# A kernel of attention and two expert mixtures: stores on GpSimd's queue, a buffer for squares, another order of weight jobs

## The chip, the cores and the metric

The kernel runs on one core of a Trainium2 chip. The metric is the time of one execution on the device in microseconds. Before the change three runs took 1863.81, 1864.39 and 1872.37 us; their median is 1864.39 us. The execution that the profiler recorded took 1853.53 us.

## The reference

Windowed attention feeds a first mixture of eight experts, in which every token goes through every expert with a weight of its own, and its result feeds a second one, in which every token goes to exactly one expert.

```python
x = attention(q, k, v)                      # 4 x 576 tokens, 8 heads of 64, window of 64
# mixture 1: N = 2304 tokens, D = 512, F = 1024, E = 8
P = exp(x @ w_gate - max)                   # then 8 rounds of row and column scaling
for e in range(E):
    out += P[:, e:e+1] * (relu(x @ w1[e]) @ w2[e])
# mixture 2: tokens are assigned greedily by logit, N / E to an expert
for e in range(E):
    mask = assigned == e
    out2[mask] = relu(out[mask] @ w1[e]) @ w2[e]
```

## The kernel before

All matmuls of the experts run in float16 pairs: each float32 value is split into a high part (ScalarE, L345, a scaled copy) and a low part (VectorE, L347, the scaled value minus the high part), and a product takes three matmuls. Weights are scaled by a power of two first. For that the sum of squares of a weight set is taken (`sum_scale`): four squares on ScalarE (L287), each over 1024 columns, whose values nobody reads and whose row sums are kept, then a matmul with ones (L302) that sums over partitions.

The stages are: attention and the first expert of mixture 1 (to about 300 us of the span), experts 1 to 7 of mixture 1 (to about 1520 us), and mixture 2 with its routing. For experts 1 to 6 the products are Strassen's: a layer 1 step (L959) is 24 matmuls against quarter weights in `w1b` and `w1x`, and a layer 2 step (L1096) is 12 matmuls against `w2b` and others. The 18 token tiles form nine pairs k; layer 2 runs two pairs behind layer 1. Of each seven products of layer 2, VectorE adds three to the output `acc` (L1072); for the other four ScalarE writes a scaled copy `y` (L1077), and twice in each pair a DMA on GpSimd's queue adds `y` to `acc` (L1079). The first of the two goes to a tile whose other half VectorE still adds to, three products later.

Between the matmuls, weights are prepared in the background. `weights_all` works through a list of jobs: the w2 and the w1 of an expert of mixture 1, and w1 or w2 of experts of mixture 2. A job squares and splits the 2 MB that four loads brought to the one buffer `raw` (L1610), stores the split parts to DRAM, from where they are loaded when their expert comes, and loads the next job's weights as parts of `raw` become free. A split or a square takes one of four buffers named `st2k` in turn and waits until the store that last read it has landed. Stores of w1 are L427 (14 of 256 KB in a job), of mixture 2's weights L473 (8), of w2 L533 (14) and, for the last expert, L498 (8).

The loads of an expert's w1 are L454, seven of 512 KB into quarter slots. Each is issued when the whole w1 of that expert has been prepared (`w1p`) and the last product of the expert before that reads the slot has been written (`w1f`). The loads of w2 (L561) follow the same rule. The x parts of a pair are L909, 896 KB.

Instructions stand on each engine in the order in which the program writes them. The background advances by ticks: every twelve matmuls of layer 1 and every six of layer 2 give 0.7 ticks, and a job asks for so many ticks between its steps: 1.2 and 0.7 for the two halves of a split (`SPW`, `LOW`), 1.5 for a square, 3.0 for the matmul behind the squares, 11 from a load to the first use. All the loads and stores named so far stand on SP's queue in program order, except L1079. A DMA whose turn has not come holds up the DMAs behind it on its queue.

Of the kernel before, what the change touches and what calls it, by code (L numbers as in the profile page):

```python
# [9 lines left out]
F16 = mybir.dt.float16  # L10
I32 = mybir.dt.int32
AF = mybir.ActivationFunctionType
# [163 lines left out]
def body(ctx, tc, dims, q, k, v, wg1, w11, w12, wg2, w21, w22, wgT, out):  # L176
# [102 lines left out]
    def sum_scale(buf, inv, sc, key=None):  # L279


        mp = small.tile([128, 8], F32, name="np8")
        e = []
        wide = not bg.hold
        for c in range(4 if wide else 0):
            a = yield Rq("ACT", 1.4, [(key, c)] if key else [], wait=1.5)
            A.activation(st2k()[:, 0:1024], buf[:, c * 1024:(c + 1) * 1024], AF.Square, accum_out=mp[:, c:c + 1])  # L287
            e.append(a.end)
        for c in range(0, 0 if wide else 8, 2):
            kd = [(key, c // 2)] if key else []  # L290
            a = yield Rq("ACT", 0.8, kd, wait=1.3)
            junk = st2k() if "pool" in rc else acc[:, NT - 2].bitcast(F16)
            s0, s1 = [buf[:, x * 512:(x + 1) * 512] for x in (c, c + 1)]
            A.activation(junk[:, 0:512], s0, AF.Square, accum_out=mp[:, c:c + 1])
            d = yield Rq("DVE", 0.77, kd, wait=0)
            V.scalar_tensor_tensor(junk[:, 512:1024], s1, 1.0, s1, op0=OP.mult, op1=OP.mult, accum_out=mp[:, c + 1:c + 2])
            e += [a.end, d.end]
        m1 = small.tile([128, 1], F32, name="m1")
        p = yield Rq("PE", 0.2, e, "psb", wait=3.0)
        pt = psb.tile([128, 512], F32, name="pb")  # L300
        k = 4 if wide else 8
        PE.matmul(pt[:, 0:k], rc["ones"], mp[:, 0:k], start=True, stop=True)  # L302
        d = yield Rq("DVE", 0.9, [p.end])
        V.tensor_reduce(m1, pt[:, 0:k], AX.X, OP.add)
        norm_pow2(m1, sc, inv)
        fl.release("psb", p.idx, d.start + 0.3)
        rc["sct"] = d.end
# [69 lines left out]
    def strassen_w1(e, sc, free):  # L377
# [31 lines left out]
        else:  # L409
# [6 lines left out]
            def out(src, name):  # L416
                o = W1N.index(name) * 2048
                for c in range(2):
                    st = []

                    def two():
                        st.append(st2k()[:, 0:1024].rearrange("p (t x) -> p t x", t=2))
                        return st[0][:, 0], st[0][:, 1]

                    yield from split_f(src[:, c], two, None, sc, 512, wait=SPW)
                    d = w1scr[e * 128:(e + 1) * 128, o:o + 2048].rearrange("p (t x) -> p t x", t=2)
                    SP.dma_start(d[:, :, c * 512:(c + 1) * 512], st[0])  # L427

            yield from comb(t3, A11, A21, OP.subtract)
            yield from out(A22, "A22")  # L430
# [29 lines left out]
    def prep_moe2(e, m, free):  # L460
        sc = wsc()
        yield from sum_scale(raw, winv[:, 2 + m, e:e + 1], sc, "job")
        for c in range(8):
            a, cc = (c % 2, c // 2) if m == 0 else (c // 4, c % 4)
            st = []

            def two():
                st.append(st2k()[:, 0:1024].rearrange("p (t x) -> p t x", t=2))
                return st[0][:, 0], st[0][:, 1]

            x, y = yield from split_f(raw[:, c * 512:(c + 1) * 512], two, None, sc, 512, pool="st2k", wait=SPW if c else 1.0)
            d = wscr[m][a][e * 128:(e + 1) * 128, :].rearrange("p (t x) -> p t x", t=2)
            SP.dma_start(d[:, :, cc * 512:cc * 512 + 512], st[0])  # L473
            fl.release("st2k", x.idx, y.end + 4.6)
            if c % 2:
                free(c // 2)
# [10 lines left out]
    def prep_w2(e, free):  # L487
        yield from sum_scale(raw, winv[:, 1, e:e + 1], w2sc, "job")
        for c in range(8):
# [5 lines left out]
                return st[0][:, 0], st[0][:, 1]  # L495

            x, y = yield from split_f(raw[:, cs], two, None, w2sc, 512, pool="st2k", wait=SPW if c else 1.0)
            SP.dma_start(w2rows(e)[:, :, cs], st[0])  # L498
            fl.release("st2k", x.idx, y.end + 4.6)
            if c % 2:  # L500
                free(c // 2)
# [2 lines left out]
    def quarters_w2(e, free):  # L504
# [14 lines left out]
        def sp(src, name):  # L519
            o = QN.index(name) * 2048  # L520
            for c in range(2):
# [8 lines left out]
                x, y = yield from split_f(src[:, 2 * c:2 * c + 2], two, None, w2sc, 512, deps=[("w2", 0)] if e == 1 else (),  # L530
                                          pool=None if e == 1 else "st2k", wait=SPW)
                d = w2scr[e * 128:(e + 1) * 128, o:o + 2048].rearrange("p (t x) -> p t x", t=2)
                SP.dma_start(d[:, :, c * 512:(c + 1) * 512], st[0])  # L533
                fl.release("st2k", x.idx, y.end + 4.6)

        yield from comb(t3, B22, B12, OP.subtract)
# [677 lines left out]

    def held_weights():
        w2g = rc["pool"].tile([128, FC, E], F32, name="w2g")
        junk = rc["pool"].tile([128, DM], F16, name="junk")
        row = []
        for e in range(E + 1):
            if e < E:  # L1220
# [374 lines left out]

    jobs = []
    m2left = [(m, x) for x in range(E) for m in range(2)]
    for e in range(1, E):
        jobs += [(1, e), (0, e)]
        for _ in range(M2PLAN.get(e, len(m2left))):  # L1600
            m, x = m2left.pop(0)
            jobs.append((2 + m, x))
# [11 lines left out]
    def weights_all():  # L1614
        for r in range(4):
            load(0, r)
        for k, (m, e) in enumerate(jobs):
# [4 lines left out]
                bg.done.add("raw2")  # L1622
                return
            yield Idle(WAIT[m])
            while m >= 2 and "T" not in rc:
                yield IDLE
            if m >= 2:
                yield from prep_moe2(e, m - 2, free)
# [48 lines left out]
    def change():  # L1677
# [5 lines left out]
        rc["ones"] = rc["pool"].tile([128, 128], F32, name="ones")  # L1683
        V.memset(rc["ones"], 1.0)
        rc["tmp"] = rc["pool"].tile([128, 2, 512], F32, name="tmp")
        mpool = mid.enter_context(tc.tile_pool(name="mpool", bufs=1))
        rc["xr"] = mpool.tile([128, 3, 2 * XO], F16, name="xr")
        w1x = mpool.tile([128, 6144], F16, name="w1x")
# [171 lines left out]
```

## Time and profile before

| what | value |
|---|---|
| median of three runs | 1864.39 us |
| profiled execution | 1853.53 us |
| its span, first to last instruction | 1851.7 us |
| mean granted TensorE clock | 0.984 of full speed |
| TensorE matmul, busy | 1764.1 us, 95% |
| VectorE, busy | 1318.2 us, 71% |
| ScalarE, busy | 1048.8 us, 57% |
| GpSimd, busy | 203.7 us, 11% |
| DMA packets of the hardware queue | 286.75 MB, 45.8% of 16 engines |
| DMA packets of GpSimd's queue | 71.33 MB, 15.6% of 16 engines |

The span is the time between the first and the last instruction of one execution; about 2 us lie around it. In the rows below, PE is TensorE's matmul side, PEld its weight loads, DVE VectorE, ACT ScalarE, POOL GpSimd and SP SyncE; a letter q behind an engine means its queue or sequencer. "out<-in" are names of the program's buffers: `ws` and `w1scr`, `w2scr` are the prepared weights in DRAM, `xr` the x parts, `in_moe_w` the weights as given.

### The profile page before, as it was taken

To read this page: it belongs to the slowest core of one execution; us is meant where nothing else is said; L and a number is where in the kernel's file an instruction comes from. 1 tells how busy PE (TensorE), PEld (TensorE's weight loads), DVE (VectorE), ACT (ScalarE), POOL (GpSimd) and SP (SyncE) were. 2 spreads that over 40 slices of the span, in tenths; PEclk is the share of its full clock that TensorE was granted. 3 is DMA by queue.
4 is the path that set the end of the run, shared out by engine and by line. 5 is a ranking of instruction groups with operands and counts; after the bars stand their busy time and mean duration, and the time that the engine had idled before them with its cause. 6 is when DMAs were issued, how large, how long until landed. Compare 5 with 4: busy or idle time off the path is not lost.

```text
span 1851.7 us, 51111 instructions
## 1 busy us (share of the span) xinstructions
PE 1764.1 (95%) x21427; PEld 1496.2 (81%) x21427; DVE 1318.2 (71%) x3129; ACT 1048.8 (57%) x2045; POOL 203.7 (11%) x268
## 2 busy tenths in 40 slices
PE   6999999998999999999999999999999999799997
PEld 5766556997899989998999899899887774577776
DVE  7888955787588778867887787678567737566640
ACT  6776335765676767677667676677643432122222
POOL 0000000000000000000010000000100102323231
PEclk9999999999999999999999999999999999799999
DMA  7353427766786997689769678986962201535460
GB/s 220 116 172 104 142 80 253 237 194 202 263 247 186 297 307 214 193 250 323 217 178 325 210 214 260 307 261 171 298 210 75 75 24 53 197 130 192 147 234 26
DMA packets 183447, 361.35 MB, mean 195 GB/s; under 512 B 15728, under 2 KB 105072, under 8 KB 179120
## 3 DMA queue, kind: packets, MB, share of 16 engines
q1 hardware_dynamic: 159984, 286.75, 45.8%
q0 software_dynamic: 23232, 71.33, 15.6%
q8 instruction: 168, 2.75, 0.6%
q14 instruction: 63, 0.52, 0.1%
HBM read 232.31 MB, written 97.40 MB: 178 GB/s over the span
## 4 chain that ended last, share of the span: by engine, by line
PE 70%; DVE 12%; DMA 12%; issue 3%; ACT 3%; SPq 0%; POOL 0%; POOLq 0%; DVEq 0%; ACTq 0%
PE p L959 14%; PE p L1096 12%; PE pb L959 10%; PE pb L1096 8%; PE p L1521 5%; PE p L1124 4%; DMA ws<-st2k 3%; PE p L1146 3%; PE p L823 3%; PE p L1507 3%; DMA raw<-in_moe_w_dram 2%; PE pb L1352 1%; DMA w2b<-w2scr 1%; DMA acc<-y 1%; DVE st2k L347 1%
## 5 line engine op out<-in xcount | busy, mean ns | idle before, releaser
L959 PEld LDWEIGHTS <-w1b 128*128 128x128 f16 x6048 | 361.5, 99 | 24.4 <-DMA w1b<-w1scr 10.3
L959 PEld LDWEIGHTS <-w1x 128*128 128x128 f16 x4536 | 270.4, 98 | 17.3 <-issue 9.7
L1096 PEld LDWEIGHTS <-hall 128*128 128x128 f16 x2268 | 214.9, 98 | 29.5 <-issue 4.7
L1096 PEld LDWEIGHTS <-xh 128*128 128x128 f16 x2268 | 214.7, 98 | 23.3 <-DVE xh L1037 1.0
L1079 POOL DMA_DIRECT2D acc<-y x108 | 93.2, 863 | 1095.3 <-ACT y L1077 672.9
L959 PE MATMUL p<-xr,w1b 128*128 128x128 f16 x3024 | 192.3, 220 | 14.3 <-DMA w1b<-w1scr 10.0
L959 PE MATMUL p<-xr,w1x 128*128 128x128 f16 x3024 | 191.2, 220 | 5.2 <-ACT xl L976 4.6
L347 DVE SCALAR_TENSOR_TENSOR st2k<-raw,wsc,st2k 128x512 f16<-128x512 f32 x200 | 148.5, 748 | 60.0 <-ACT st2k L345 57.3
L959 PE MATMUL pb<-xr,w1b 128*128 128x128 f16 x3024 | 190.3, 219 | 0.0
L345 ACT ACTIVATE st2k<-raw,wsc 128x512 f16<-128x512 f32 x200 | 140.0, 713 | 53.2 <-DMA ws<-st2k 41.3
L979 DVE TENSOR_TENSOR xl<-pb,xl 128x512 f32<-128x512 f32 x126 | 86.7, 688 | 92.7 <-PE pb L959 80.1
L1077 ACT ACTIVATE y<-p,SE 128x256 f32<-128x256 f32 x216 | 101.3, 469 | 82.4 <-PE p L1096 76.5
L287 ACT ACTIVATE st2k<-raw 128x1024 f16<-128x1024 f32 x108 | 113.5, 1052 | 43.9 <-DMA raw<-in_moe_w_dram 17.2
L1072 DVE SCALAR_TENSOR_TENSOR acc<-pb,SE,acc 128x256 f32<-128x256 f32 x162 | 77.9, 481 | 61.8 <-PE pb L1096 38.6
L1124 PE MATMUL p<-w2b,hall 128*128 128x512 f16 x432 | 107.1, 384 | 0.0
L823 PE MATMUL p<-xh,w1b 128*128 128x384 f16 (+1 forms) x512 | 99.7, 286 | 3.6 <-DVE w1b L347 1.6
L976 ACT ACTIVATE xl<-p 128x512 f32<-128x512 f32 x126 | 74.3, 590 | 50.5 <-PE p L959 50.5
L959 PE MATMUL pb<-xr,w1x 128*128 128x128 f16 x1512 | 94.8, 219 | 3.3 <-ACT xl L976 3.3
L1146 PE MATMUL p<-w2b,hall 128*128 128x512 f16 x432 | 97.2, 379 | 0.0
L823 PEld LDWEIGHTS <-w1b 128*128 128x128 f16 x768 | 63.2, 98 | 36.1 <-issue 3.9
L1096 PE MATMUL p<-w2b,hall 128*128 128x256 f16 x648 | 79.7, 273 | 5.6 <-ACT y L1077 3.3
L1096 PE MATMUL p<-w2b,xh 128*128 128x256 f16 x648 | 81.6, 275 | 0.3 <-DVE xh L1033 0.3
(322 smaller groups left out, 3323.0 us busy)
## 6 DMA issues: line engine op xcount, KB each, us to landing
raw<-in_moe_w_dram SPq DMA_DIRECT2D x128, 512.0 KB, 7.2
xr<-xtd SPq DMA_DIRECT2D x63, 896.0 KB, 6.5
ws<-st2k SPq DMA_DIRECT2D x128, 256.0 KB, 6.3
acc<-y POOLq DMA_DIRECT2D x108, 256.0 KB, 6.2
w1scr<-st2k SPq DMA_DIRECT2D x84, 256.0 KB, 2.8
w2scr<-st2k SPq DMA_DIRECT2D x78, 256.0 KB, 4.0
w2b<-w2scr SPq DMA_DIRECT2D x28, 512.0 KB, 8.3
w1b<-w1scr SPq DMA_DIRECT2D x24, 512.0 KB, 9.7
```

The lines of the kernel that those rows point to most:

```text
L287: A.activation(st2k()[:, 0:1024], buf[:, c * 1024:(c + 1) * 1024], AF.Square, accum_out=mp[:, c:c + 1])
L345: A.activation(hi, src, AF.Copy, scale=sc)
L347: V.scalar_tensor_tensor(lo, src, sc, hi, op0=OP.mult, op1=OP.subtract)
L823: PE.matmul(p[:, 0:w], w1v[wi][:, c, fs], x[:, c, ts], start=(n == 0), stop=(n == 3 * DC - 1))
L959: PE.matmul(bank[:, fs], aq[wi][:, c, fs], xq[xi][:, c], start=(start and f == 0 and m == 0), stop=(m == 5), skip_group_check=True)
L979: V.tensor_tensor(t, bank, t, OP.add)
L1077: A.activation(y[:, h * hd:(h + 1) * hd], bank[:, 0:hd], AF.Copy, scale=SE[:, e, i:i + 1])
L1079: G.dma_start(acc[:, i], y, accum_op=OP.add)
L1096: PE.matmul(bank[:, 0:hd], hq[hi][:, c], wv[wi][:, c], start=(pool is not None and m == 0), stop=(m == 11), skip_group_check=True)
L1124: PE.matmul(s[0], h[hi].rearrange("p (c t) -> p c t", c=4)[:, f % 4], w2v[wi][:, f], start=(f == 0 and hi == wi == 0), stop=(f == FC - 1 a ...
L1146: PE.matmul(p, h[:, f, js], w2v[wi][:, f], start=(n == 0), stop=(n == 3 * FC - 1))
L1521: PE.matmul(p[:, 0:CAP], wv2[f // 4][w][:, f % 4, dsl], x[:, f], start=(n == 0), stop=(n == 3 * FC - 1))
```

## The change

Every store of prepared weights is issued on GpSimd's queue in place of SP's, 304 DMAs. The squares of a job write one buffer `junk` of their own in place of an `st2k` buffer, and the matmul behind them is asked for 3.6 ticks later in place of 3.0. The scratch of the last expert's gate products (`held_weights`) takes the first tile of `y` in place of memory of its own. The list of jobs is ordered anew: it begins with w2 and w1 of experts 1 and 2, and then each expert's share of mixture 2's jobs follows w2 and w1 of the expert after it. The test that keeps mixture 2's jobs from starting before the shared buffers exist now holds for every job from the third on.

```diff
@@ sum_scale
-            A.activation(st2k()[:, 0:1024], buf[:, c * 1024:(c + 1) * 1024], AF.Square, accum_out=mp[:, c:c + 1])
+            A.activation(rc["junk"], buf[:, c * 1024:(c + 1) * 1024], AF.Square, accum_out=mp[:, c:c + 1])
...
-        p = yield Rq("PE", 0.2, e, "psb", wait=3.0)
+        p = yield Rq("PE", 0.2, e, "psb", wait=3.6)
@@ strassen_w1
-                    SP.dma_start(d[:, :, c * 512:(c + 1) * 512], st[0])
+                    G.dma_start(d[:, :, c * 512:(c + 1) * 512], st[0])
@@ prep_moe2
-            SP.dma_start(d[:, :, cc * 512:cc * 512 + 512], st[0])
+            G.dma_start(d[:, :, cc * 512:cc * 512 + 512], st[0])
@@ prep_w2
-            SP.dma_start(w2rows(e)[:, :, cs], st[0])
+            G.dma_start(w2rows(e)[:, :, cs], st[0])
@@ quarters_w2
-                SP.dma_start(d[:, :, c * 512:(c + 1) * 512], st[0])
+                G.dma_start(d[:, :, c * 512:(c + 1) * 512], st[0])
@@ held_weights
-        junk = rc["pool"].tile([128, DM], F16, name="junk")
+        junk = rc["y"][:, 0].bitcast(F16)[:, 0:DM]
@@ the list of jobs
+    jobs += [(1, 1), (0, 1)]
     for e in range(1, E):
-        jobs += [(1, e), (0, e)]
+        if e < E - 1:
+            jobs += [(1, e + 1), (0, e + 1)]
@@ weights_all
-            while m >= 2 and "T" not in rc:
+            while k >= 2 and "T" not in rc:
@@ change
+        rc["junk"] = rc["pool"].tile([128, 1024], F16, name="junk")
```

On SP, at the boundary from expert 1 to expert 2 of mixture 1, before (L1610 loads raw, L454 loads the next w1):

```order
L427 DMA w1scr<-st2k 128x2x512 x6
L909 DMA xr<-xtd 128x3584
L427 DMA w1scr<-st2k 128x2x512 x8
L1610 DMA raw<-in_moe_w_dram 128x1024 x4
L454 DMA w1b<-w1scr 128x2048 x2
L454 DMA w1x<-w1scr 128x2048
L454 DMA w1b<-w1scr 128x2048
L454 DMA w1x<-w1scr 128x2048 x2
L454 DMA w1b<-w1scr 128x2048
L909 DMA xr<-xtd 128x3584
```

and at the same place after the change (raw is now loaded in L1612):

```order
L1612 DMA raw<-in_moe_w_dram 128x2x512 x3
L909 DMA xr<-xtd 128x3584
L454 DMA w1b<-w1scr 128x2048 x2
L454 DMA w1x<-w1scr 128x2048
L454 DMA w1b<-w1scr 128x2048
L1612 DMA raw<-in_moe_w_dram 128x2x512
L454 DMA w1x<-w1scr 128x2048
L1612 DMA raw<-in_moe_w_dram 128x2x512
L454 DMA w1x<-w1scr 128x2048
L454 DMA w1b<-w1scr 128x2048
```

The stores of that w1 are gone from SP, and its loads no longer stand behind them and four raw loads, but among the raw loads of a later job.

On GpSimd, all of experts 1 to 6 of mixture 1, before (`mmg` is the maximum that starts the gates, L1204 a subtraction of the last expert's stage):

```order
L268 ISA mmg<-m1g 128x1
L1079 DMA acc<-y 128x512 x108
L1204 ISA
L1204 TENSOR_TENSOR st2k<-tmp,st2k 128x512 x8
L1233 ISA
```

and after the change, of the same stretch only the work of expert 1 up to its seventh pair:

```order
L533 DMA w2scr<-st2k 128x2x512 x6
L1079 DMA acc<-y 128x512
L533 DMA w2scr<-st2k 128x2x512 x5
L1079 DMA acc<-y 128x512
L533 DMA w2scr<-st2k 128x2x512 x3
L1079 DMA acc<-y 128x512 x2
L427 DMA w1scr<-st2k 128x2x512 x2
L1079 DMA acc<-y 128x512
L427 DMA w1scr<-st2k 128x2x512 x4
L1079 DMA acc<-y 128x512
L427 DMA w1scr<-st2k 128x2x512 x4
L1079 DMA acc<-y 128x512
```

Two to six stores now stand between one acc<-y and the next, where none stood.

On ScalarE, at a job's last split and first squares, before (np holds the row sums, `w2sc` and `wsc` a scale):

```order
L345 ACTIVATE st2k<-raw,wsc 128x512
L973 ACTIVATE xl<-p_9527 128x512
L287 ACTIVATE st2k,np_9834<-raw 128x1024
L1077 ACTIVATE y<-p_9564,SE 128x256
L287 ACTIVATE st2k,np_9834<-raw 128x1024
```

and after:

```order
L345 ACTIVATE st2k<-raw,w2sc 128x512
L1077 ACTIVATE y<-p_9843,SE 128x256
L976 ACTIVATE xl<-p_10155 128x512
L287 ACTIVATE junk,np_10152<-raw 128x1024
L1077 ACTIVATE y<-p_10182,SE 128x256
```

The squares stand where they stood between evacuations, but they write `junk` and no buffer that a store reads.

## Rows read from the trace of the kernel before

**Rows 1.** First part of the page: busy us (share of the span) xinstructions.
```profile
PE 1764.1 (95%) x21427; PEld 1496.2 (81%) x21427; DVE 1318.2 (71%) x3129; ACT 1048.8 (57%) x2045; POOL 203.7 (11%) x268
```

**Rows 2.** Table by stretches: stretch, us, busy of each engine, PEclk, DMA share, GB/s.
```profile
300.00:454.40 154.40, 152.03 (x2120) 143.53 (x2118) 120.91 (x193) 105.80 (x175) 11.46 (x13) 1.00 0.70 211
454.40:464.40 10.00, 0.01 (x1) 0.01 (x1) 0.79 (x1) 0.47 (x1) 0.86 (x1) 0.76 0.97 319
464.40:470.00 5.60, 5.60 (x42) 4.86 (x43) 0.00 (x0) 0.86 (x2) 0.00 (x0) 0.51 1.03 421
470.00:475.00 5.00, 5.00 (x71) 4.73 (x68) 3.67 (x6) 3.44 (x6) 0.00 (x0) 1.00 0.67 272
475.00:1370.00 895.00, 874.24 (x11766) 824.99 (x11764) 679.51 (x1082) 624.94 (x1043) 80.83 (x94) 1.00 0.80 246
```

**Rows 3.** Waits of TensorE: waiter <- releaser: us in total, times, longest.
```profile
PE p L959 <- DMA w1b<-w1scr: 10.0, 1, 10.0
...
PE pb L302 <- ACT st2k L287: 5.9, 4, 2.1
...
PE pb L1096 <- DVE xh L1037: 0.7, 1, 0.7
```

**Rows 4.** SP's timeline at the first boundary: start us, us, instruction, count.
```profile
452.97 1.90 SPq L1610 DMA_DIRECT2D raw<-in_moe_w_dram  x4
454.96 1.03 SPq L454 DMA_DIRECT2D w1b<-w1scr  x2
```

**Rows 5.** ScalarE's timeline in three places; in brackets its idle time before.
```profile
1028.22 0.72 ACT L345 ACTIVATE st2k<-raw,wsc 128x512 f16<-128x512 f32 x1 [4.99 <-DMA ws<-st2k]
...
1326.55 0.72 ACT L345 ACTIVATE st2k<-raw,wsc 128x512 f16<-128x512 f32 x1 [5.32 <-DMA ws<-st2k]
...
688.17 1.06 ACT L287 ACTIVATE st2k<-raw 128x1024 f16<-128x1024 f32 x1 [3.38 <-issue]
```

**Rows 6.** TensorE's timeline in the same three places.
```profile
1032.31 1.95 PE L959 MATMUL p<-xr,w1x 128*128 128x128 f16 x23 [3.89 <-ACT xl L976]
...
1331.93 1.25 PE L1096 MATMUL p<-w2b,hall 128*128 128x256 f16 x10 [3.30 <-ACT y L1077]
...
689.85 1.33 PE L959 MATMUL pb<-xr,w1x 128*128 128x128 f16 x21 [2.56 <-ACT xl L976]
```

**Rows 7.** Fifth part of the page: groups, busy us, mean ns | idle before, releaser.
```profile
L347 DVE SCALAR_TENSOR_TENSOR st2k<-raw,wsc,st2k 128x512 f16<-128x512 f32 x200 | 148.5, 748 | 60.0 <-ACT st2k L345 57.3
...
L345 ACT ACTIVATE st2k<-raw,wsc 128x512 f16<-128x512 f32 x200 | 140.0, 713 | 53.2 <-DMA ws<-st2k 41.3
```

**Rows 8.** The stores of line L473, all 128.
```profile
DMA to landing us min/median/max: 2.4/6.3/11.6
```

**Rows 9.** Sixth part of the page: DMA issues, KB each, median us to landing.
```profile
acc<-y POOLq DMA_DIRECT2D x108, 256.0 KB, 6.2
w1scr<-st2k SPq DMA_DIRECT2D x84, 256.0 KB, 2.8
w2scr<-st2k SPq DMA_DIRECT2D x78, 256.0 KB, 4.0
```

**Rows 10.** SP's timeline from 402 to 407 us.
```profile
402.66 0.50 SPq L909 DMA_DIRECT2D xr<-xtd  x1
403.25 2.38 SPq L533 DMA_DIRECT2D w2scr<-st2k  x3
405.69 1.12 SPq L1610 DMA_DIRECT2D raw<-in_moe_w_dram  x2
```

**Rows 11.** The chain that ended last, from 404 to 419 us: start, us, what.
```profile
407.34 10.12 DMA acc<-y
```

**Rows 12.** Instructions of the tile y: count, ns min/median/max, first and last start.
```profile
L1079 POOL DMA_DIRECT2D acc<-y x108: 850/859/1175, 335.8 to 1362.1; - x108
```

**Rows 13.** Waits, columns as in rows 3, of VectorE.
```profile
DVE acc L1072 <- DMA acc<-y: 20.9, 12, 5.9
```

**Rows 14.** VectorE's timeline near 1342 us.
```profile
1342.28 0.48 DVE L1072 SCALAR_TENSOR_TENSOR acc<-pb,SE,acc 128x256 f32<-128x256 f32 x1 [5.91 <-DMA acc<-y]
```

## The prediction, made before the result was known

> **What bounds the kernel now.** I read the page's first part, then the stage table, then who TensorE waited for, and last the stretches around its longest waits. TensorE is busy for 1764.1 us, 95% of the span [rows 1], so what a change in the background work can win is TensorE's idle time, and what it can lose is more of it. The changed code works between about 300 us, where the first expert is done, and 1370 us. There the stage table leaves TensorE idle for 2.4 + 10.0 + 20.8 = 33.1 us [rows 2]. I find three causes worth a term.
>
> First, one wait of 10.0 us for the next expert's w1 [rows 3]. SP issues the four raw loads of the following job at 452.97 us and all seven w1 loads only behind them, from 454.96 us on [rows 4]; TensorE does next to nothing from 454.4 to 464.4 us. It then starts slow: the granted clock is 0.51 from 464.4 to 470 us, which is the 1.2 GHz level, after ten idle microseconds, and 42 matmuls run in those 5.60 us, where the next 5.00 us hold 71 [rows 2]. At 71 in 5.00 us, 5.60 us would have held 79.5; the missing 37.5 cost 37.5 / 14.2 = 2.6 us more, so this place costs 12.6 us.
>
> Second, waits in which ScalarE was held by the four st2k buffers. At 1028.22 us a split had waited 4.99 us for a store to land, at 1326.55 us another 5.32 us [rows 5], and TensorE lost 3.89 and 3.30 us behind them [rows 6]. At 688.17 us it was a square that came 3.38 us late [rows 5]; TensorE lost 2.56 us [rows 6]. The profile names no releaser for that square; I take it to be a buffer too, because it writes st2k right behind the splits of the job before. Together 9.75 us.
>
> Third, 5.9 us in four waits of the matmul that sums a weight set's squares (L302) for its last square [rows 3].
>
> **Part 1: the next expert's w2 and w1 are prepared one expert ahead.** Both job lists hold the same jobs and the same bytes. What moves is when w1 of expert 2 is ready: in the order of SP its seven loads now stand among the loads of x and raw, each as soon as its slot is free, as those of the later experts did before. The later boundaries show no wait for w1 [rows 3], so I book all 12.6 us. The lower bound is about 5 us: the sixteen DMA engines were 0.97 busy in that stretch [rows 2], and the same bytes still have to pass near the boundary.
>
> **Part 2: squares write a buffer of their own.** A square no longer waits for a store, so the 2.56 us at 688 us go (0 if that wait had another cause), and the first four splits of a job find four buffers that nothing has touched during the squares. It costs nothing: the same four instructions on the same engine. The PE step behind them is asked for 0.6 ticks later (3.6 for 3.0). A step of 24 matmuls of L959 and 12 of L1096 is 2.8 ticks; 11766 matmuls in 895 us [rows 2] make 13.1 a microsecond, 36 of them 2.74 us and a tick 0.98 us. That gives each of the four L302 waits 0.59 us, 2.4 us in all. Raw loads that stand behind fewer stores, and squares that are not held, may take the rest of the 5.9. I book 4.0 us, between 2.4 and 5.9.
>
> **Part 3: 304 stores go from SP's queue to GpSimd's.** When does a buffer stall ScalarE? Splits of a job are 1.9 ticks apart (1.2 + 0.7 asked for in the code), 1.86 us. A split needs the buffer of the fourth store before it. That store was issued 0.71 + 0.75 us after its own split began [rows 7], and the new split wants to begin 4 x 1.86 = 7.4 us after that, so a store may take some 6 us to land. The stores to ws take 2.4, 6.3 and 11.6 us (shortest, median, longest) [rows 8], those to w1scr and w2scr 2.8 and 4.0 us in the middle [rows 9]. So mixture 2's stores are the ones that stall, in the bursts of loads.
>
> Does GpSimd's queue bring them through such a burst? The nearest row is the accumulating DMA of y, which has that queue to itself: 6.2 us in the middle [rows 9], no better. At 407.34 us one is issued behind an x load, three stores and two raw loads of the previous five microseconds [rows 10], and lands 10.12 us later [rows 11]. So another queue is not a free lane. The two buffer stalls that hang on landing are worth 3.89 + 3.30 = 7.2 us; the gain is between 0 and 7.2, and I take half, 3.6 us: the y row is near the bad end, but a store ahead of the loads is not behind all of them.
>
> The Trainium skill says otherwise (DMA: Bandwidth & Descriptors, Queues, rings and completion order): each DMA engine takes packets from its queues in turn, so a store on a queue of its own would pass waiting loads. By that rule the whole 7.2 us would be won; the row at 407.34 us speaks against it.
>
> What it costs stands on GpSimd. In the order the 108 acc<-y DMAs stood in one row; now one to six stores stand between most of them, and each store waits for VectorE's split. Issuing one acc<-y takes 0.86 us in the middle and at most 1.18 [rows 12], the nearest row for a store of the same bytes. GpSimd is then busy for 0.86 of each 1.86 us, so an acc<-y that comes at any time waits 0.46 x 0.43 = 0.2 us on average, and at most for one split and its issue, 0.71 + 0.75 + 0.86 = 2.3 us. It may also lie behind a store in the queue, up to the 2.4 us that the shortest one takes. So it lands 0.2 to 4.7 us later; I take 2. Half of them, 54, are read again by VectorE three products on (L1072). That wait is now 20.9 us in 12 cases, the longest 5.9 us [rows 13], and of all this TensorE shows one wait of 0.7 us [rows 3], behind the 5.91 us at 1342.28 us [rows 14]. If the cases double and each grows by 2 us, VectorE waits 24 x 2 + 20.9 = 69 us, 48 more; at 0.7 in 20.9 TensorE loses 2 us, at 0.7 in 5.9 it loses 6. I take 4, and 0 to 12 for the range.
>
> Software descriptors can be held up by VectorE, says the Trainium skill (SBUF — State Buffer, SBUF: two separate sides): in its two-port modes VectorE locks GpSimd out of the port they share, and the descriptors of a DMA wait. By that rule a store's issue would grow, the sum would lose all of part 3's gain, and the slower rival below would come near; but the 108 issues of rows 12 lie between 0.85 and 1.18 us beside a VectorE that is busy for 679.5 of 895 us [rows 2], so the sum goes by the rows.
>
> **Small parts, at nothing.** Fourteen of the stores belong to the first job, before 300 us; eight stand ahead of GpSimd's all-reduce that starts the gates, 8 x 0.86 = 6.9 us at most, and the gates are asked for only at the third token pair of expert 1. SP's queue loses stores that waited for VectorE; its x loads never held TensorE there. The scratch for the last expert's gate products moves to y, whose last DMA lies before. The reload of raw for these products comes some 16 ticks later; in VectorE's order six evacuations of L979 are left behind the last of them, where eight were left before, all ahead of the routing.
>
> **Sum.** 12.6 + 2.6 + 4.0 + 3.6 - 4 = 18.8 us off the profiled execution: 1853.5 - 18.8 = 1834.7 us. That execution lies 10.9 us below the median of the three runs, 1864.4 us, so I scale: 1864.4 x (1 - 18.8 / 1853.5) = 1845.5, say 1845 us. Bounds: all gains and no cost, 12.6 + 2.6 + 5.9 + 7.2 = 28.3, give 1836; the lower ends, 5 + 0 + 2.4 + 0 - 12 = -4.6, would give 1869, but for all of them at once there is little chance.
>
> **Rivals.**
> - The queue brings nothing: stores still lie behind loads. For it: the 10.12 us. Then 12.6 + 2.6 + 2.4 - 4 = 13.6 us, 1851 us.
> - The stores do pass the loads, and acc<-y is hardly hurt: 28.3 - 2 = 26.3 us, 1838 us. For it only that GpSimd's queue has held one DMA at a time, so the trace shows no stream of stores on it. This is the time by the rule on queues in the Trainium skill.
> - The boundary stays bound by the transfer: loads, raw and stores near 454 us fill the DMA engines, half of the 12.6 us comes back, and the stores cost 8: 6.3 + 2.6 + 4.0 + 2.0 - 8 = 6.9 us, 1857 us. Here the change would not do what it says. Against it: no such wait at five later boundaries.
> - Slower: acc<-y becomes the bound. Place: L1072 behind each of the 54 reads. If acc<-y lands at about 12 us instead of 6.2, each read waits as the one at 1342.28 us did, and each costs TensorE 0.7 us: 54 x 0.7 = 38 us against 22.8 us of gains, 15 us slower, 1880 us. It decides from a delay of some 5 us on nearly every one; my upper bound is 4.7.
>
> **Chances.** Forecast (1845 us) 0.42, queue brings nothing 0.22, stores pass 0.17, transfer bound 0.11, slower 0.08. About 0.5%, 9.3 us, is what a measurement of this kernel can tell from no change. Faster by more needs under 1855 us: nearly all of the first three cases and a part of the fourth, 0.78; within 0.5% 0.14; slower 0.08. The range 1830 to 1860 us takes in the first four cases, with a few us for the scatter of the runs, and leaves out the slower one and some of its neighbours.
>
> **What would show it.** Right: no wait for w1b near 454 us and a full clock through 475 us; squares that never wait for a store; L302 waits under 3 us in sum; TensorE idle for 14 to 18 us between 300 and 1370 us. The landing of ws stores tells the first two rivals apart: about 3 us in the bursts if they pass the loads, 8 to 10 if not. Wrong: waits of L1072 for acc<-y well over 70 us, or issues on GpSimd far longer than 0.9 us; then part 3 costs more than I booked.

## The result, and the profile after

The changed kernel took 1841.0 us in the median of four runs, beside 1868.4 us for the kernel before on the same chip: a ratio of 0.9856, 95% interval 0.9823 to 0.9889, or 27 us. Forecast were 1845 us, a ratio of 0.9899. The size is near, and sign and range hold; the way there was in part another. From the first matmul of L1477, early in mixture 2, to the end, four records of one set of runs need 277 to 279 us, the first record of the changed kernel 275, and all others 262 to 269, whatever the kernel. So whole times are compared only with the kernel before beside them, and traces only up to that point.

The first part of the page after, beside [rows 1]: the same matmuls, less idle time, and GpSimd's busy time doubled by the issues of 304 stores.

```profile
PE 1761.5 (96%) x21427; PEld 1492.6 (81%) x21427; DVE 1320.4 (72%) x3129; ACT 1047.3 (57%) x2045; POOL 430.3 (23%) x572
```

The table of stretches, with the columns and bounds of [rows 2]:

```profile
300.00:454.40 154.40, 146.43 (x2010) 137.16 (x2009) 111.57 (x178) 98.95 (x168) 38.03 (x49) 0.99 0.67 206
454.40:464.40 10.00, 10.00 (x141) 9.52 (x139) 7.76 (x12) 5.50 (x8) 3.49 (x5) 1.00 0.94 296
464.40:470.00 5.60, 5.60 (x77) 5.30 (x76) 3.72 (x5) 3.67 (x7) 2.51 (x4) 1.00 1.02 379
470.00:475.00 5.00, 5.00 (x71) 4.76 (x70) 4.69 (x8) 4.78 (x9) 0.58 (x1) 1.00 1.04 345
475.00:1370.00 895.00, 883.60 (x11894) 833.32 (x11893) 685.89 (x1098) 625.83 (x1046) 262.75 (x340) 1.00 0.79 251
1370.00:1490.00 120.00, 120.00 (x1297) 91.09 (x1296) 85.66 (x259) 47.74 (x89) 13.85 (x11) 1.00 0.25 70
```

The wait at the boundary to expert 2 is gone: no idle time and a full clock through 475 us. From 300 to 1370 us TensorE idles for 8.0 + 11.4 = 19.4 us in place of 33.1; 14 to 18 were forecast. The first row got worse: 8.0 us idle where there were 2.4. And the last row, a stretch in which I had booked nothing, has no idle time at all; the kernel before has 4.5 us there, and a clock of 0.97:

```profile
1370.00:1490.00 120.00, 115.54 (x1238) 89.10 (x1238) 82.64 (x250) 41.78 (x78) 9.64 (x9) 0.97 0.29 89
```

TensorE's 21427 matmuls stand in nearly the same order in all the kernels, so two traces can be set side by side by counting them. This table, worked out from the start times of the matmuls with these numbers, gives for each stretch how many us more (+) or less (-) than the first record of the kernel before it took:

```
                    3100-  4600-  4900-  9500- 10000- 16400-   sum
                    4600   4900   9500  10000  16400  18800
before, 2nd record   0.3   -1.0    1.5    0.5   -0.6   -3.5   -2.7
after                8.8  -12.8   -0.5   -5.0   -6.3   -9.1  -24.9
after, 2nd record    8.3  -12.8   -0.4   -5.0   -3.6   -7.5  -21.1
```

Columns: 3100 to 4600 is most of expert 1 (327 to 447 us), 4600 to 4900 the boundary to expert 2, 16400 to 18800 the last expert with its gate products, up to the routing. A second record of the same kernel differs by up to 3.5 us in a column. So one stretch lost 8 to 9 us, and the rest won 29 to 34.

**Where it lost.** The stretch from 327 to 447 us, of the kernel before, of the changed one, and of its second record:

```profile
327.00:447.00 120.00, 120.00 (x1635) 113.91 (x1633) 98.05 (x153) 86.89 (x146) 11.46 (x13) 1.00 0.71 211
```

```profile
327.00:447.00 120.00, 113.89 (x1513) 106.92 (x1511) 89.91 (x136) 79.15 (x134) 36.09 (x47) 0.99 0.68 205
```

```profile
327.00:447.00 120.00, 114.58 (x1523) 107.17 (x1521) 89.96 (x137) 79.69 (x135) 36.16 (x47) 0.99 0.69 207
```

122 matmuls fewer, at 1635 in 120 us, are 9.0 us. The longest wait there, of the changed kernel, on TensorE, ScalarE, GpSimd's and SP's queue:

```profile
358.46 2.72 PE L959 MATMUL p<-xr,w1x 128*128 128x128 f16 x24 [2.46 <-ACT xl L976]
...
355.22 0.72 ACT L345 ACTIVATE st2k<-raw,w2sc 128x512 f16<-128x512 f32 x1 [4.80 <-DMA w2scr<-st2k]
...
346.09 0.72 POOL L533 DMA_DIRECT2D w2scr<-st2k  x1 [0.54 <-DVE st2k L347]
...
344.55 1.59 SPq L1612 DMA_DIRECT2D raw<-in_moe_w_dram  x2
346.24 0.43 SPq L909 DMA_DIRECT2D xr<-xtd  x1
```

The split at 355.22 us takes the buffer of the fourth split before it, whose store was issued at 346.09 us. The buffer came free only when the split could start, some 9 us later: two raw loads and an x load, 1.9 MB, had gone out on SP's queue about then. An evacuation stood behind the split, TensorE waited 2.46 us for it, and its next 24 matmuls took 2.72 us where 24 take 1.50 at the full clock (the granted clock is 0.53 from 358 to 361 us). Over all, ScalarE's waits for buffers grew. Its waits from 300 to 1370 us, before:

```profile
ACT st2k L345 <- DMA ws<-st2k: 41.3, 25, 5.3
...
ACT st2k L345 <- DMA w2scr<-st2k: 8.8, 6, 3.6
...
ACT st2k L345 <- DMA w1scr<-st2k: 0.7, 1, 0.7
```

and after (us in total, times, longest):

```profile
ACT st2k L345 <- DMA ws<-st2k: 43.3, 26, 3.8
ACT st2k L345 <- DMA w2scr<-st2k: 33.3, 19, 4.8
...
ACT st2k L345 <- DMA w1scr<-st2k: 13.9, 11, 2.8
```

50.8 us have become 90.5. With order and squares but all stores on SP's queue (two records further down) the same three rows come to 55.8 and 55.1 us, so most of the rise is the stores' move. VectorE's wait for acc<-y, on which I had put the cost of the stores (20.9 us in [rows 13]), hardly moved:

```profile
DVE acc L1072 <- DMA acc<-y: 27.9, 14, 5.2
```

**Where it won beyond the forecast.** Two waits of the kernel before in the last expert, on VectorE and TensorE:

```profile
1376.61 0.69 DVE L1226 SCALAR_TENSOR_TENSOR junk<-raw,st2k 128x512 f16<-128x512 f32 x1 [7.31 <-DMA st2k<-in_moe_w_gateT_dram]
...
1377.53 1.59 PE L1187 MATMUL pb<-wg2s,xT 128*128 128x8 f32 x8 [2.00 <-DVE lgh L1188]
...
1488.76 0.15 DVE L256 TENSOR_SCALAR pb<-mm 128x1 int32<-128x1 int32 x1 [6.13 <-POOL mm L1233]
...
1490.55 2.72 PE L959 MATMUL p<-xr,w1b 128*128 128x128 f16 x24 [3.01 <-DVE xl L979]
```

VectorE stands in front of the first gate product for 7.3 us until its row of weights has landed, and in front of the all-reduce's result for 6.1 us; other work of TensorE waits behind it each time and then runs at a lower clock (0.60 from 1377 to 1381 us, 0.57 from 1490 to 1494). In the changed kernel neither wait exists.

### The profile page after: what moved, and what is told of

Read it like the earlier page. It is cut to its first block, busy times and chain, and to the rows that moved or that the text cites. A ratio compares the mean times of both kernels' runs of the same rounds, so it can differ in the third digit from the quotient of the medians.

```text
span 1836.5 us, 51168 instructions
## 1 busy us (share of the span) xinstructions
PE 1761.5 (96%) x21427; PEld 1492.6 (81%) x21427; DVE 1320.4 (72%) x3129; ACT 1047.3 (57%) x2045; POOL 430.3 (23%) x572
## 3 DMA queue, kind: packets, MB, share of 16 engines
q1 hardware_dynamic: 77296, 207.04, 34.1%
q0 software_dynamic: 47552, 151.04, 27.1%
## 4 chain that ended last, share of the span: by engine, by line
PE 61%; issue 12%; DVE 10%; DMA 9%; POOL 3%; ACT 3%; another core or an unknown queue 1%; POOLq 0%; SPq 0%; ACTq 0%; DVEq 0%
PE p L959 12%; PE p L1096 9%; PE pb L959 8%; PE pb L1096 6%; PE p L1521 5%; PE p L1124 4%; DMA ws<-st2k 4%; PE p L823 3%; PE p L1146 3%; PE p L1507 3%; DMA raw<-in_moe_w_dram 2%; DMA w2scr<-st2k 2%; PE pb L1352 1%; POOL w2scr L533 1%; POOL acc L1079 1%
## 5 line engine op out<-in xcount | busy, mean ns | idle before, releaser
L959 PEld LDWEIGHTS <-w1b 128*128 128x128 f16 x6048 | 358.4, 98 | 11.3 <-issue 2.6
L959 PEld LDWEIGHTS <-w1x 128*128 128x128 f16 x4536 | 270.3, 98 | 19.4 <-issue 11.8
L959 PE MATMUL p<-xr,w1x 128*128 128x128 f16 x3024 | 190.9, 220 | 7.8 <-ACT xl L976 7.6
L959 PE MATMUL p<-xr,w1b 128*128 128x128 f16 x3024 | 189.5, 219 | 1.9 <-DVE xl L979 1.9
L959 PE MATMUL pb<-xr,w1b 128*128 128x128 f16 x3024 | 189.7, 219 | 0.0
L1079 POOL DMA_DIRECT2D acc<-y x108 | 101.3, 938 | 273.7 <-ACT y L1077 241.1
L473 POOL DMA_DIRECT2D ws<-st2k x128 | 93.4, 732 | 209.8 <-DVE st2k L347 182.5
L1072 DVE SCALAR_TENSOR_TENSOR acc<-pb,SE,acc 128x256 f32<-128x256 f32 x162 | 77.8, 480 | 62.9 <-PE pb L1096 30.5
L287 ACT ACTIVATE junk<-raw 128x1024 f16<-128x1024 f32 x108 | 113.3, 1049 | 16.4 <-DMA raw<-in_moe_w_dram 16.3
L533 POOL DMA_DIRECT2D w2scr<-st2k x70 | 52.8, 755 | 214.3 <-DVE st2k L347 210.6
L959 PE MATMUL pb<-xr,w1x 128*128 128x128 f16 x1512 | 95.0, 219 | 1.3 <-ACT xl L976 1.2
L427 POOL DMA_DIRECT2D w1scr<-st2k x84 | 62.8, 748 | 130.7 <-DVE st2k L347 124.3
```

The source lines that it names most:

```text
L287: A.activation(rc["junk"], buf[:, c * 1024:(c + 1) * 1024], AF.Square, accum_out=mp[:, c:c + 1])
L473: G.dma_start(d[:, :, cc * 512:cc * 512 + 512], st[0])
L959: PE.matmul(bank[:, fs], aq[wi][:, c, fs], xq[xi][:, c], start=(start and f == 0 and m == 0), stop=(m == 5), skip_group_check=True)
L1079: G.dma_start(acc[:, i], y, accum_op=OP.add)
```

## The experiments

Each kernel is the one before or the changed one with some parts of the change. The ratios are to the kernel before beside it.

| kernel | median us | ratio, 95% interval |
|---|---|---|
| new order alone | 1850.2 | 0.9885 (0.9839 to 0.9931) |
| stores alone | 1856.8 | 0.9906 (0.9873 to 0.9940) |
| stores alone, again | 1841.4 | 0.9923 (0.9895 to 0.9951) |
| squares alone | 1862.4 | 0.9955 (0.9936 to 0.9973) |
| order and squares | 1839.8 | 0.9825 (0.9778 to 0.9872) |
| order and squares, again | 1824.0 | 0.9820 (0.9796 to 0.9845) |
| all three, again | 1828.8 | 0.9849 (0.9829 to 0.9869) |
| order, squares, mixture 2's stores | 1832.1 | 0.9872 (0.9853 to 0.9890) |
| order, squares, mixture 1's stores | 1830.1 | 0.9851 (0.9829 to 0.9874) |
| order and squares, 3.0 ticks | 1842.4 | 0.9914 (0.9888 to 0.9941) |
| order and squares, 4.2 ticks | 1829.7 | 0.9862 (0.9835 to 0.9889) |
| the kernel before, again | 1858.2 | 1.0011 (0.9995 to 1.0028) |

The columns of the matmul table for them:

```
                    3100-  4600-  4900-  9500- 10000- 16400-   sum
                    4600   4900   9500  10000  16400  18800
order alone          1.9  -12.9    7.2   -5.7    1.1   -6.1  -14.5
stores alone         4.6   -3.6    0.5   -0.8   -4.2   -3.4   -6.9
  again              3.1   -4.8    1.0   -0.7   -3.1   -5.4   -9.9
squares alone        0.2    1.5    4.6   -4.5    0.9  -10.9   -8.2
order and squares    0.4  -12.9   -1.0   -3.0   -5.4   -7.6  -29.6
  again              0.5  -12.9    1.6   -1.0   -5.7  -10.6  -28.0
  + mixture 2 stores 2.1  -12.8    0.3   -1.6   -0.8   -8.6  -21.3
  + mixture 1 stores 5.8  -12.8    3.4   -5.2   -8.2   -9.1  -26.1
  3.0 ticks          1.7  -12.8    9.9   -5.7    1.5   -0.9   -6.3
  4.2 ticks          2.2  -12.9    7.4   -5.7   -6.1   -9.0  -24.2
```

### The order alone

```diff
+    jobs += [(1, 1), (0, 1)]
     for e in range(1, E):
-        jobs += [(1, e), (0, e)]
+        if e < E - 1:
+            jobs += [(1, e + 1), (0, e + 1)]
...
-            while m >= 2 and "T" not in rc:
+            while k >= 2 and "T" not in rc:
```

> The kernel before with the new list of jobs alone; stores stay on SP's queue and squares in st2k. Theory A (the order is what wins): the 12.6 us at the boundary to expert 2 go, and so do the two waits of the last expert's gate products near 1376 and 1488 us with the half clock behind them, 5.5 + 4.7 = 10.2 us, because those products come later in the order of VectorE. That is 22.8 us, 1868 - 23 = 1845 us. Theory B (the order needs the stores off SP's queue): w1's loads still stand behind stores that wait for VectorE, TensorE still waits 3 to 10 us for w1b near 454 us, and the time is 1855 us or more.

The ratio was 0.9885, 22 us, near theory A's 22.8, but its record shows only 14.5 us of that up to the routing. The boundary went with it, 12.9 us, with the stores where they were, so theory B falls. But the two waits of the gate products did not go: they stand in this trace with 1.9 us (L1187) and 2.9 us (L959). Behind them the granted clock is 1.00 here (1367 to 1375 and 1477 to 1485 us), so in this record they cost only that idle time. And L302 got worse, 10.3 us in six waits where [rows 3] has 5.9 in four:

```profile
PE pb L302 <- ACT st2k L287: 10.3, 6, 4.8
...
PE pb L1187 <- DVE lgh L1188: 1.9, 1, 1.9
```

### The stores alone

```diff
-                    SP.dma_start(d[:, :, c * 512:(c + 1) * 512], st[0])
+                    G.dma_start(d[:, :, c * 512:(c + 1) * 512], st[0])
```

and the other three lines in the same way.

> The kernel before with the 304 stores on GpSimd's queue and nothing else. Theory A (a store behind loads lands no sooner on another queue): no gain at the st2k waits and some cost by new ones, as the 8.7 us that TensorE loses in expert 1 of the changed kernel: 1866 to 1877 us. Theory C (the stores pass the loads, and loads pass the stores that wait for VectorE): both st2k waits at 1028 and 1328 us go, 7.2 us, and w1 is loaded earlier at 454 us: 1861 us or less.

> The kernel before with only its stores moved, a second time: it was timed 13 us faster than before, but its record up to mixture 2's routing is only 6 us ahead. Theory C (in the old order the stores' move does clear the way for loads): ratio 0.992 to 0.996, the wait for w1b 6 to 7 us in place of 10, 2 to 5 us lost in expert 1. Rival (the first ratio was right): 0.990 or less. Rival (nothing): 0.998 or more.

0.9906 and 0.9923: in the old order the move is worth 14 to 18 us by the times, which is theory C's. The two records show 6.9 and 9.9 us of it up to the routing; where the rest lies they do not show. The second record has these gains: w1b is waited for 6.3 us in place of 10.0, L302 for 1.8 in place of 5.9, and the first wait of the gate products no longer reaches TensorE. Each hangs on loads that used to stand behind stores on SP's queue. Theory C's other term did not come: in the second record the splits at 1024.61 and 1317.37 us still wait 5.41 and 3.51 us for stores to ws. Expert 1 loses 3 to 5 us here too.

### The squares alone

```diff
-            A.activation(st2k()[:, 0:1024], buf[:, c * 1024:(c + 1) * 1024], AF.Square, accum_out=mp[:, c:c + 1])
+            A.activation(rc["junk"], buf[:, c * 1024:(c + 1) * 1024], AF.Square, accum_out=mp[:, c:c + 1])
...
-        p = yield Rq("PE", 0.2, e, "psb", wait=3.0)
+        p = yield Rq("PE", 0.2, e, "psb", wait=3.6)
```

and the gate products' scratch in `y`.

> The kernel before with squares written to the unread buffer, the matmul behind them asked for at 3.6 ticks, and the gate products' scratch in y. Theory A: the wait of 2.56 us at 688 us goes, and the four L302 waits lose at least 2.4 of their 5.9 us: 4 to 7 us faster, 1861 to 1864 us. Rival: the square at 688 us was late for another reason, and freeing the buffers for splits only moves the wait on: 1866 to 1868 us.

1862.4 us, a ratio of 0.9955 or 8 us: inside theory A's time, but not by its terms. L302 is still waited for 6.0 us, and near the place of the wait at 688 us TensorE now waits 4.4 us behind a split that itself waits for a store. The wait has moved on, as the rival has it:

```profile
692.57 0.72 ACT L345 ACTIVATE st2k<-raw,wsc 128x512 f16<-128x512 f32 x1 [4.71 <-DMA ws<-st2k]
```

The boundary did not get better (12.3 us of waiting for w1b), and a later one, at 990.85 us, now costs 5.3 us, with the w1 loads behind four raw loads there too. But the two stalls behind splits at 1028 and 1328 us are gone. The largest column of the table is the last, 10.9 us: both waits of the gate products are gone. So it is this part, not the order, that took them away.

### Order and squares, no store moved

The changed kernel with its four lines of stores back on SP.

> The changed kernel with its 304 stores back on SP's queue: order and squares alone. Theory A (stores neither win nor cost in sum): 1841 us, as the changed kernel, without the 8.7 us that it loses in expert 1, and with st2k waits of up to 5 us elsewhere in their place. Rival 1 (the stores cost what expert 1 loses): 1832 us, faster than the changed kernel. Rival 2 (the stores are what clears the boundary and the st2k waits): 1848 us or more.

> The kernel with the new order and the squares' buffer but all stores on SP's queue, recorded and timed a second time, in more rounds. Theory A (the stores' move is worth nothing once order and squares are there, and costs expert 1 its 6 to 9 us): a ratio of 0.982 to 0.985, at or under the changed kernel's two, 0.9856 and 0.9849; nothing lost in expert 1. Rival (its first ratio of 0.9825 was luck and the move of the stores is worth some us): 0.987 or more.

0.9825 and 0.9820. The first measurement does not decide its text: 1839.8 us is near theory A's 1841, and its interval holds both that and rival 1's 1832 (ratios 0.9854 and 0.9805 of 1868.4 us). The second is theory A of its text, and its interval leaves out 0.9854. Without the stores' move the kernel is faster by some 5 us (0.9820 to 0.9849 of 1857 us); the intervals overlap, but both pairs point the same way, and so do the records, 28.0 and 29.6 us won up to the routing against 21.1 and 24.9. Expert 1 loses nothing:

```profile
327.00:447.00 120.00, 119.93 (x1629) 113.65 (x1627) 95.50 (x151) 85.99 (x144) 11.49 (x13) 1.00 0.76 225
```

The stalls behind splits at 1028 and 1328 us, 3.9 and 3.3 us, are not in this trace either, so the move is not needed for that; near the first, L302 now waits 3.4 us for a square. This is the fastest kernel found, 1824.0 us where the one before took 1856.9.

### The kernel before, and the changed one, recorded again

No edit.

> The kernel before, unchanged, recorded a second time. Five recorded kernels need 278 to 280 us from the routing of mixture 2 to the end, the first record of the kernel before 265 us. Theory A (that record was a lucky execution): its end takes 278 us now, the execution 1866 us, and the stretch up to there is as in the first record within 3 us. Rival (the five changes each cost 13 us at the end): 265 us again, 1853 us.

> The changed kernel, unchanged, recorded a second time. Theory A (stores on GpSimd's queue cost in expert 1, every time): TensorE loses 6 to 10 us between 327 and 447 us again, the two waits at the last expert's gate products stay away, ratio 0.985. Rival (the 8.7 us was one execution's accident): under 3 us there, and the rest as before.

The kernel before is the same as itself (1.0011). Counted from the first matmul of L1477, its end takes 263.8 us in this record and 265.2 in the first. That end was no luck of the first record, as theory A had it. Nor do the changes cost 13 us there: the changed kernel's second record has 261.6 us, its first had 275.1. It goes with the set of runs; why is open. The 8 to 9 us in expert 1 came again, as theory A said.

### The stores by kind

Order and squares, with this line alone, and in the second kernel the other three without it:

```diff
-            SP.dma_start(d[:, :, cc * 512:cc * 512 + 512], st[0])
+            G.dma_start(d[:, :, cc * 512:cc * 512 + 512], st[0])
```

> New order, squares in their own buffer, and of the stores only the 128 of mixture 2's weights on GpSimd's queue; the 176 of mixture 1 stay on SP's. Theory A (a store keeps its place ahead of the loads only on their own queue, and the cost in expert 1 is that of w2's and w1's stores): no loss in expert 1, so 1832 to 1838 us, at or under the kernel with no store moved (1840 us). Rival (mixture 2's stores, the slow ones, are what the move hurts): 1840 to 1848 us.

> The same with the other part: the 176 stores of mixture 1's w2 and w1 on GpSimd's queue, the 128 of mixture 2 on SP's. Theory A: the 7 to 9 us in expert 1 are lost again, 1844 to 1850 us. Rival (the cost in expert 1 has nothing to do with these stores): 1840 us or less.

Expert 1, with mixture 2's stores moved and with mixture 1's:

```profile
327.00:447.00 120.00, 118.47 (x1601) 111.85 (x1599) 93.75 (x148) 84.17 (x142) 17.28 (x21) 1.00 0.75 222
```

```profile
327.00:447.00 120.00, 115.39 (x1567) 108.59 (x1565) 91.74 (x139) 82.01 (x139) 30.50 (x39) 1.00 0.69 209
```

34 and 68 matmuls fewer than before, 2.5 and 5.0 us: in that stretch it is more the stores of w2 and w1, as theory A said, though less than the 7 to 9 us that it gave. Its times were wrong. The kernel with mixture 1's stores moved has 0.9851, where its 1844 to 1850 us are 0.9870 or more of 1868.4; it is as fast as the changed kernel. Moving mixture 2's stores alone costs 0.5% against no move (0.9872 to 0.9820). Splits wait 51.2 us for ws there, 30.2 with all stores on SP. The rival is right on that. Whether moving them alone is worse than moving all (0.9849) is not shown: the intervals overlap.

These two kernels also show the landing times of the stores, which the first page of the changed kernel does not list. Part 6 with mixture 1's stores on GpSimd's queue:

```profile
raw<-in_moe_w_dram SPq DMA_DIRECT2D x128, 512.0 KB, 6.4
xr<-xtd SPq DMA_DIRECT2D x63, 896.0 KB, 6.9
...
w1scr<-st2k POOLq DMA_DIRECT2D x84, 256.0 KB, 4.4
w2scr<-st2k POOLq DMA_DIRECT2D x78, 256.0 KB, 5.8
w2b<-w2scr SPq DMA_DIRECT2D x28, 512.0 KB, 5.9
```

and with all on SP's (second record):

```profile
raw<-in_moe_w_dram SPq DMA_DIRECT2D x128, 512.0 KB, 6.5
xr<-xtd SPq DMA_DIRECT2D x63, 896.0 KB, 7.4
...
w1scr<-st2k SPq DMA_DIRECT2D x84, 256.0 KB, 3.0
w2scr<-st2k SPq DMA_DIRECT2D x78, 256.0 KB, 4.8
w2b<-w2scr SPq DMA_DIRECT2D x28, 512.0 KB, 7.2
```

Stores land 1.0 and 1.4 us later, these loads 0.1 to 1.3 us sooner (of the others, `w1x` 0.3 us later). The changed kernel's second record agrees: its stores of w1 and w2 land in 4.4 and 5.8 us, those to ws in 6.1, where they take 5.2 with all on SP's. One place in expert 1 shows why. With all stores on SP's queue (first record):

```profile
326.16 2.28 SPq L533 DMA_DIRECT2D w2scr<-st2k  x3
328.53 1.11 SPq L909 DMA_DIRECT2D xr<-xtd  x1
```

The x load stands behind three stores, each of which waits for its split, and the stores of that stretch land in 3.3 to 4.9 us. With mixture 1's stores on GpSimd's queue, SP's and GpSimd's timelines:

```profile
328.61 0.32 SPq L909 DMA_DIRECT2D xr<-xtd  x1
...
328.68 1.45 POOL L533 DMA_DIRECT2D w2scr<-st2k  x2 [5.92 <-DVE st2k L347]
```

and the DMA queues of the same kernel from 328.6 to 332.7 us, packets, MB and share of 16 engines:

```profile
DMA packets 105, 0.76 MB, mean 186 GB/s; under 512 B 0, under 2 KB 0, under 8 KB 104
## 3 DMA queue, kind: packets, MB, share of 16 engines
q1 hardware_dynamic: 104, 0.75, 72.3%
q8 instruction: 1, 0.02, 1.9%
```

The load goes out first. In the four microseconds after the store's issue the load's queue, q1, moves 0.75 of its 0.9 MB and the stores' queue, q0, moves nothing, though both issues were over at 330.13 us. That is no fixed delay of that queue: the quickest store of the same kernel on it lands in 2.5 us. The stores of that stretch land in a median of 6.7 us and at most 7.3, and the split at 336.06 us has waited 2.7 us for one. Here the queue of its own did not let stores pass loads; it let loads pass stores.

### The matmul behind the squares at 3.0 and at 4.2 ticks

```diff
-        p = yield Rq("PE", 0.2, e, "psb", wait=3.6)
+        p = yield Rq("PE", 0.2, e, "psb", wait=3.0)
```

> The same with the matmul behind the squares asked for after 3.0 ticks again: the squares' buffer without the later matmul. Theory D (the 0.6 ticks, summed over the jobs, put the first product of the last expert's gate weights behind the loads that it needs): the waits at PE matmul 16782 (2.0 us) and 17928 (2.9 us) and the half clock behind them come back, and L302 waits grow by up to 0.6 us each: 7 to 12 us slower than the kernel with 3.6 ticks, ratio 0.987 to 0.990. Rival (the squares' buffer or the scratch in y moved them): those waits stay away, and the time is within 3 us.

> The same with 4.2 ticks. If the L302 waits that are left (7.4 us in the first record of this kernel) fall by 0.6 us in each of the four, and nothing else moves: 2 us faster than with 3.6, ratio 0.981. Rival: the jobs end so late that the gate products, 28 places later in the order of VectorE, run into the routing: slower by 3 us or more.

At 3.0 ticks the ratio is 0.9914, 17 us worse than at 3.6, where theory D's upper end was 12. Its mechanism is there, with the squares' buffer and the scratch in y left in: VectorE's and TensorE's timelines at the gate products.

```profile
1368.70 0.69 DVE L1226 SCALAR_TENSOR_TENSOR y<-raw,st2k 128x512 f16<-128x512 f32 x1 [7.25 <-DMA st2k<-in_moe_w_gateT_dram]
...
1369.63 1.59 PE L1187 MATMUL pb<-wg2s,xT 128*128 128x8 f32 x8 [1.94 <-DVE lgh L1188]
...
1482.85 2.40 PE L959 MATMUL p<-xr,w1b 128*128 128x128 f16 x21 [3.21 <-DVE xl L979]
```

The first product starts when TensorE has done 16782 matmuls, as in the kernel before; with 3.6 ticks, 16810: it then stands directly behind the last split on VectorE, where eight instructions lay between them at 3.0 ticks, and meets no wait. The rest of the loss lies between matmuls 4900 and 9500 (9.9 us where the two records at 3.6 have -1.0 and 1.6; a 4.6 us wait of L302 at 473.66 us with the lower clock behind it) and between 10000 and 16400. 4.2 ticks are slower than 3.6 by 0.4%, and neither of the two texts has the reason: the gate products still meet no wait at their start, but L302 waits 4.4 us at 688.36 us. So 3.6 is not a better margin for one matmul; it is another arrangement of all the jobs.

## Why the prediction was right, and where its steps were not

**The boundary, 12.6 us booked.** 12.8 and 12.9 us in all records with the new order, whatever else is changed. The step and its price hold, with the matmuls at the lower clock counted in; the rival of the transfer bound falls.

**The square at 688 us, 2.6 us booked.** The changed kernel wins 3.0 us between matmuls 7700 and 7900 in both records, but the buffer is not what wins it. The order alone wins 2.6 us there, since other work stands at that place; the squares' part alone loses 3.2, since a split waits for a store where the square did. What I took for granted about that square is borne out: before the change ScalarE's squares wait 10.9 us with no releaser named, and no kernel whose squares have their own buffer has such a wait.

**L302, 4.0 us booked.** 5.9 us have become 2.2:

```profile
PE pb L302 <- ACT junk L287: 2.2, 4, 1.3
```

The size is right and the cause is only in part. I booked 2.4 us for the 0.6 ticks and let squares that are not held, and raw loads behind fewer stores, add the rest. With order, squares and 3.6 ticks but the stores on SP, L302 waits 7.7 and 8.3 us, more than before; with nothing but the stores moved, 2.6 and 1.8. So the gain belongs to the stores' move, to which I had given the smaller share. The squares' own wait for raw goes some way with it (35.0 us with stores on SP, 3.3 with the stores moved alone, 16.3 in the changed kernel) but is not the whole of it, since the kernel before has 17.2. The 0.6 ticks are worth 3.3 us (11.6 at 3.0 ticks, 8.3 at 3.6).

**The landing of stores, 3.6 us booked.** The two stalls that this term priced at 7.2 us are both gone in the changed kernel, but not by the stores' move: they are gone with order and squares, and with the squares' part alone, and stay as shorter ones with the stores alone. On landing itself the move brings a loss. The stores to ws in the changed kernel's second record (the 112 of 128 whose landing the trace gives), beside [rows 8]:

```profile
DMA to landing us min/median/max: 2.5/6.1/10.9
```

Three of them in a burst of loads near 1300 us take 8.5 to 10.9 us, which I had given as the sign that stores do not pass the loads. So on landing the rival "the queue brings nothing" was right. My bound "between 0 and 7.2" had no place for a loss, though I had the two halves of it in hand: that an issue behind loads lands late (10.12 us in [rows 11]), and that SP's loads would no longer stand behind stores. I put the second on the side of gains alone. By the rule of the Trainium skill (DMA: Bandwidth & Descriptors, Queues, rings and completion order) each DMA engine takes packets in turn from the queues that it has work for. The trace of the kernel with mixture 1's stores moved shows q0 without a packet for 4 us after its stores' issue, while q1 moved 0.75 MB; whether q0 had work ready then, it does not show. So the rule gave no price for a store's landing here, and the time that I worked out by it, 1838 us, came near for other reasons.

**What it costs on GpSimd, 4 us booked.** Landing and cost together came to 3.6 - 4 = 0.4 us lost in my sum; the stores' move in the full kernel loses about 5, with its gain at L302 already in that. And it loses them at another place. L1072 waits 27.9 us (32.1 in the second record) where I expected 69. The cost is splits that wait for buffers in expert 1, and I named no such place: from 327 to 360 us the trace of before holds twelve stores to ws, and the new order brings twelve stores of w2 there. A store's issue takes 0.73 to 0.78 us in the mean, under the 0.86 that I took from [rows 12].

**At nothing: the gate products.** This is the step that fell furthest. I asked of the later reload only whether it still ends ahead of the routing, and had bounded the changed work to 300 to 1370 us. VectorE's waits of 7.31 and 6.13 us a little later are in the trace of before, and 0.6 ticks decide whether they are there. Their price varies: TensorE idles 5 us behind them, and the lower clock adds to that in some records and not in others. The last column has 0 to -6.1 us in the four records with both waits (the kernel before twice, the order alone, 3.0 ticks) and -7.5 to -10.9 in the eight with neither. Without this gain of some 5 to 10 us the change would have won 17 to 22 us, about the forecast.

So the sum was near partly by luck: a gain that I missed stood against a loss that I missed, and the gains at 688 us, of the two stalls and of L302 came from other parts of the change than those I booked them to. The forecast of the sum, 18.8 us, has 27 beside it. The boundary, which could be read from one row with one answer, held in cause and size; the parts that hung on what is late next did not.

**What is left open.** Where the stores' move in the old order wins the part of its 14 to 18 us that the traces up to the routing do not show, what keeps q0 without a packet behind a load, and how much of the 17 us for the 0.6 ticks is chance of this arrangement.

## What to carry to other kernels

On one in-order queue the program order is also a priority: a store ahead of a load goes first (4.1 us to landing in the median at the place shown, 6.7 on a queue of its own). Here moving stores to another queue freed the loads, not the stores, so do it where loads are late (14 us or more won in the old order by the times, 7 to 10 of them seen in the traces) and not where the stores' buffers are (5 us lost in the new one). When a change shifts work by a fraction of a step, read every in-order wait downstream of it, to the end of the program, as carefully as the place that was edited.

## What the runs showed of the hardware

The same bytes move in other packets on the two queues. Part 3 of the page after:

```profile
q1 hardware_dynamic: 77296, 207.04, 34.1%
q0 software_dynamic: 47552, 151.04, 27.1%
```

Before, q1 had 159984 packets and q0 23232. The 79.7 MB of stores were 82688 packets on SP's queue, about 1 KB each, and are 24320 on GpSimd's, about 3.3 KB; the DMA engines' time is nearly the same, 45.8% + 15.6% before and 34.1% + 27.1% after. Larger packets brought no time back here.
